# A new hand-written order for the 1648 operations of an attention and gated feed-forward kernel

## The chip, the core and the metric

The kernel runs on one core of a Trainium2 chip. The core has five engines that each work through a queue of their own, in order: TensorE (PE, matrix products; PEld is its loading of weights), VectorE (DVE), ScalarE (ACT), GpSimd (POOL) and SyncE (SP, which here only issues transfers). They wait for one another through semaphores. The metric is the device time of one execution in microseconds. The kernel before takes 346.71 us (median of 3 runs, 345.82 to 346.75).

## The reference

```
for c in range(nc):                                   # 24 chunks of 32 queries
    q_c = q[:, :, c_start:c_end]
    k_full = concat([mem_k, k[:, :, l_start:r_end]])  # 8 memory keys, 16 left, 32 own, 8 right
    scores = scale * matmul(q_c, k_full.T)
    a = exp(scores - max);  a = a / (sum(a) + 1e-9)
    out[:, :, c_start:c_end] = matmul(a, v_full)
x = out, heads joined                                 # (4, 768, 512)
h = maximum(x @ w_in, 0)                              # (4, 768, 1024)
conv = sum over k of conv_w[k] * h shifted by k - 1   # three taps along the sequence
y = (h * sigmoid(conv)) @ w_out                       # (4, 768, 512)
```

Four batches of 768 positions, 8 heads of 64. The weights arrive as 64-bit floats; every product of the feed-forward part is made of three products of a high and a low part, so that it has nearly the precision of fp32.

## The kernel before, in words

The work is cut into 1648 operations. Function `op` of class `Plan` records each with what it reads and writes; the functions below it (`from_f64`, `attention`, `ffn_in`, `gated`, `sums`, `weight_sums`, `seven`, `ffn_out`) only make operations. At the end `run` goes through the list `ORDER` and issues them in exactly that order. Each engine gets its operations in the order in which the list names them, so the one list sets all five queues, and it also decides which buffer a tile gets: a tile takes the first free slot of its pool at its first use, and gives it back after its last.

- `from_f64` (L296 to L364) turns one block of 64-bit weights into a high and a low fp32 part, on ACT, DVE and partly POOL. It has run 17 times when all weights are there.
- `attention` runs 32 times (4 batches, 2 halves of the sequence, 4 pairs of heads). PE makes the scores (L397, tile `s`), DVE takes their maximum (L406, tile `top`). Then either DVE subtracts it (L411) and ACT takes the exponential (L417), or ACT scales the maximum (L428) and takes six exponentials with it as a bias (L432). DVE sums (L444) and inverts (L446), DVE or POOL multiplies (L449). The result is turned, either by PE (L461) or by DVE and a trip through DRAM (L479, tile `t_dram`); ACT copies it (L468), PE multiplies it with v (L508, tile `ta`), and ACT and DVE split that into high and low parts (L511, L514).
- `ffn_in` is 64 times four groups of three PE products (L530, tile `f`), with a copy by ACT (L540) that applies the maximum with zero.
- `gated` is 32 times the three taps (ACT L551 or DVE L555, then DVE L560 twice), a tanh on ACT (L564), the product with h (DVE L569, or ACT L573 and POOL L574), and the split of the result (ACT L586, then DVE or POOL L589).
- `ffn_out` makes 18 of the 24 output tiles: 24 PE products each (L727), a copy by ACT (L738) and a store. The last batch goes another way: `sums` and `weight_sums` prepare sums of its operands and of the output weights (L596, L644), and `seven` makes seven block products in place of eight (L680, L698).

`weight_sums` is ten operations on POOL at L596, numbers 1298 to 1307 in the list, each over 128x1024 elements. They can run as soon as all of w_out is converted, and they are needed only by the last batch.

Of the kernel before, what the change touches and what calls it, by code (L numbers as in the profile page):

```python
# [46 lines left out]
    581, 582, 570, 571, 12, 587, 588, 583, 584, 11, 14, 28, 572, 573, 29, 585, 576, 592, 574, 45, 46, 589, 575, 15,  # L47
    16, 586, 17, 31, 63, 62, 13, 48, 79, 598, 32, 30, 80, 577, 33, 18, 19, 34, 20, 21, 22, 47, 602, 64, 35, 578,
    579, 36, 65, 593, 96, 590, 49, 23, 37, 50, 38, 97, 580, 24, 39, 51, 594, 595, 52, 53, 54, 40, 131, 25, 41, 66,
    67, 596, 82, 599, 591, 42, 26, 68, 69, 600, 27, 130, 597, 43, 601, 70, 756, 71, 612, 44, 739, 603, 114, 83, 55,  # L50
    773, 56, 58, 113, 740, 622, 57, 72, 73, 147, 165, 604, 605, 606, 607, 84, 608, 75, 74, 774, 757, 85, 81, 76,
    59, 609, 86, 60, 87, 99, 148, 88, 77, 610, 133, 61, 758, 775, 98, 100, 613, 101, 741, 134, 78, 166, 135, 89,
    90, 618, 619, 611, 791, 792, 92, 643, 91, 102, 632, 136, 793, 794, 742, 795, 116, 115, 614, 615, 759, 103, 616,
    617, 620, 104, 621, 743, 0, 776, 105, 106, 132, 808, 809, 810, 811, 623, 628, 117, 118, 119, 624, 120, 107,
    108, 150, 629, 625, 200, 626, 630, 137, 151, 93, 631, 812, 199, 138, 649, 139, 627, 140, 218, 168, 109, 110,
    94, 358, 111, 95, 287, 760, 121, 826, 122, 112, 169, 827, 828, 829, 141, 778, 183, 123, 633, 124, 143, 777,
    634, 635, 125, 126, 170, 638, 813, 182, 814, 796, 797, 830, 127, 1, 636, 2, 637, 152, 142, 144, 217, 393, 202,
    153, 639, 154, 640, 641, 128, 129, 145, 146, 642, 203, 744, 171, 745, 235, 644, 645, 3, 4, 779, 780, 149, 5,
    650, 6, 7, 204, 155, 8, 9, 646, 205, 647, 172, 206, 815, 816, 156, 781, 782, 798, 173, 817, 207, 648, 799, 800,
    157, 208, 158, 10, 209, 159, 201, 185, 186, 651, 652, 220, 236, 187, 818, 801, 210, 211, 783, 746, 221, 831,  # L60
    832, 833, 174, 222, 802, 803, 161, 761, 762, 763, 819, 784, 820, 188, 189, 804, 160, 764, 747, 748, 749, 765,
    175, 252, 805, 167, 176, 253, 834, 867, 868, 664, 238, 835, 836, 162, 849, 862, 184, 239, 288, 844, 845, 163,
    377, 766, 178, 837, 863, 213, 846, 847, 767, 190, 191, 864, 865, 177, 848, 179, 750, 192, 212, 240, 255, 290,
    322, 271, 665, 821, 850, 851, 869, 675, 430, 241, 242, 768, 180, 769, 852, 270, 243, 870, 340, 342, 164, 949,
    256, 853, 244, 181, 866, 223, 871, 193, 195, 666, 950, 272, 751, 219, 838, 257, 670, 305, 785, 671, 224, 289,
    194, 1002, 1003, 324, 214, 752, 258, 196, 822, 215, 273, 259, 341, 245, 216, 197, 854, 872, 985, 986, 198, 225,
    274, 880, 881, 786, 839, 246, 951, 676, 823, 952, 953, 323, 260, 667, 1004, 226, 882, 306, 681, 227, 228, 229,
    840, 275, 883, 673, 884, 1005, 682, 375, 987, 897, 988, 668, 677, 678, 679, 248, 261, 291, 989, 262, 292, 293,
    263, 237, 931, 898, 932, 230, 684, 294, 295, 264, 855, 276, 277, 278, 231, 254, 899, 841, 900, 933, 296, 787,
    279, 280, 1006, 247, 934, 343, 325, 376, 753, 683, 326, 249, 360, 232, 250, 344, 914, 327, 233, 915, 265, 916,  # L70
    251, 685, 901, 359, 234, 281, 770, 328, 885, 886, 935, 266, 919, 283, 856, 345, 329, 412, 330, 672, 771, 331,
    917, 297, 298, 308, 346, 857, 282, 267, 674, 653, 361, 858, 268, 284, 309, 299, 918, 332, 285, 333, 334, 824,
    362, 363, 990, 991, 269, 286, 481, 347, 348, 394, 669, 954, 955, 411, 654, 364, 788, 301, 956, 957, 992, 349,
    920, 300, 887, 655, 888, 889, 890, 310, 311, 873, 921, 659, 336, 993, 350, 902, 903, 904, 656, 905, 906, 335,
    351, 302, 657, 907, 660, 874, 661, 658, 958, 891, 892, 396, 378, 697, 337, 922, 908, 303, 698, 967, 968, 662,
    994, 875, 972, 973, 859, 410, 969, 365, 312, 366, 970, 974, 975, 663, 313, 314, 338, 893, 352, 315, 703, 1007,
    339, 316, 704, 699, 1008, 1009, 772, 429, 971, 894, 976, 923, 463, 307, 936, 318, 317, 379, 380, 937, 397, 398,
    381, 382, 959, 354, 876, 353, 938, 428, 383, 413, 355, 399, 384, 385, 386, 400, 1010, 304, 939, 940, 395, 414,
    415, 1011, 1124, 401, 356, 941, 1020, 416, 464, 367, 368, 319, 357, 466, 320, 700, 701, 431, 321, 686, 692,
    1089, 680, 960, 687, 1021, 693, 369, 705, 371, 402, 706, 924, 1022, 1141, 387, 370, 445, 482, 1090, 702, 1091,  # L80
    909, 961, 389, 719, 432, 1023, 433, 417, 688, 1092, 1093, 388, 1125, 1126, 1024, 842, 1127, 1055, 1056, 535,
    1057, 1012, 962, 390, 418, 419, 446, 448, 720, 942, 420, 910, 943, 372, 1013, 1058, 1037, 421, 1128, 963, 877,
    391, 449, 422, 860, 1059, 1072, 1038, 403, 392, 404, 1073, 450, 406, 721, 722, 373, 944, 964, 945, 725, 925,
    1039, 1040, 806, 405, 374, 708, 499, 1106, 1107, 946, 1108, 1109, 1074, 423, 695, 1014, 689, 789, 790, 690,
    1075, 1015, 434, 467, 694, 1142, 1143, 1144, 407, 1076, 424, 425, 408, 1016, 484, 1145, 707, 1041, 426, 1129,
    1130, 427, 409, 1111, 995, 807, 1060, 1061, 451, 911, 825, 1017, 723, 691, 843, 1062, 1063, 696, 1112, 1064,
    996, 452, 1110, 724, 453, 1113, 1131, 1132, 1133, 1025, 1114, 926, 1115, 468, 754, 729, 1094, 1095, 755, 1096,
    1097, 454, 1026, 455, 435, 436, 714, 1027, 1028, 1077, 1368, 1029, 735, 927, 726, 1098, 928, 437, 727, 1078,
    485, 456, 457, 1079, 1146, 977, 978, 730, 1030, 486, 438, 709, 710, 517, 736, 1042, 487, 1043, 1044, 731, 732,
    1045, 711, 1080, 895, 712, 439, 1046, 728, 878, 518, 1147, 440, 713, 733, 1148, 1369, 1370, 1149, 1388, 737,  # L90
    738, 1371, 488, 861, 447, 997, 1081, 1378, 1389, 458, 516, 459, 469, 470, 471, 441, 734, 1116, 472, 1379, 1380,
    1381, 1382, 979, 498, 1150, 715, 717, 519, 520, 716, 718, 1298, 460, 442, 483, 501, 1390, 1391, 521, 522, 523,
    524, 525, 1392, 1383, 1384, 1358, 1359, 1117, 465, 998, 879, 929, 1099, 999, 473, 1118, 502, 503, 474, 461,
    475, 476, 1372, 462, 1385, 553, 526, 1373, 1299, 1300, 1386, 489, 527, 1360, 1361, 1362, 1363, 1364, 504, 505,
    1365, 506, 1100, 1031, 1366, 490, 1032, 1374, 1398, 1348, 1349, 534, 980, 477, 981, 1399, 1400, 443, 491, 1401,
    1402, 1350, 1375, 1151, 1403, 1101, 552, 444, 1387, 1152, 1065, 492, 1367, 1376, 493, 1351, 965, 528, 555, 478,
    494, 495, 529, 537, 530, 1153, 1176, 507, 508, 1033, 1066, 1352, 1404, 1405, 1353, 1354, 1082, 966, 1377, 479,
    947, 1102, 1177, 509, 538, 539, 1406, 1407, 496, 540, 541, 480, 1281, 1178, 556, 948, 1119, 497, 896, 912,
    1355, 557, 1083, 1084, 510, 512, 982, 1356, 983, 984, 1393, 1394, 1134, 913, 1047, 1048, 558, 559, 1135, 1228,
    1179, 1229, 1230, 1282, 1283, 542, 543, 536, 1103, 511, 1180, 560, 1159, 1160, 1395, 1161, 1120, 1121, 1231,  # L100
    1000, 1284, 1085, 1162, 1163, 1086, 500, 561, 562, 513, 1285, 1232, 531, 1396, 1397, 544, 1246, 1247, 563, 930,
    564, 1248, 1438, 1193, 514, 1357, 1210, 545, 546, 1049, 1211, 1249, 515, 1212, 1439, 1440, 1154, 1050, 1441,
    1442, 1194, 1443, 1051, 565, 1155, 1067, 1250, 1018, 566, 1195, 1001, 532, 1052, 1196, 1264, 1265, 1266, 1267,
    1197, 548, 554, 1444, 1418, 533, 1268, 1136, 1156, 1301, 1419, 1420, 1137, 567, 547, 549, 1304, 550, 1019,
    1445, 1138, 551, 568, 569, 1198, 1421, 1068, 1213, 1199, 1446, 1251, 1200, 1201, 1214, 1447, 1202, 1215, 1216,
# [759 lines left out]
```

## Time and profile before

| | |
|---|---|
| median of 3 runs | 346.71 us |
| the profiled execution | 346.62 us, its span 344.8 us |
| mean granted clock of TensorE | 0.995 |
| PE busy | 328.1 us, 95% of the span |
| DVE busy | 279.3 us, 81% |
| ACT busy | 209.7 us, 61% |
| POOL busy | 117.4 us, 34% |

PE has work in nearly all of the span. A matrix product is counted busy from its start to its end, and products overlap, so PE's busy time says less than the distance from one start to the next. Where a row ends in square brackets, they hold the idle time of the engine just before the instruction and what ended it. The durations of DVE and POOL hold the time in which an instruction had begun and stood still.

### The profile page before, as it was taken

To read this page: it belongs to the slowest core of one execution; us is meant where nothing else is said; L and a number is where in the kernel's file an instruction comes from. 1 tells how busy PE (TensorE), PEld (TensorE's weight loads), DVE (VectorE), ACT (ScalarE), POOL (GpSimd) and SP (SyncE) were. 2 spreads that over 40 slices of the span, in tenths; PEclk is the share of its full clock that TensorE was granted. 3 is DMA by queue.
4 is the path that set the end of the run, shared out by engine and by line. 5 is a ranking of instruction groups with operands and counts; after the bars stand their busy time and mean duration, and the time that the engine had idled before them with its cause. 6 is when DMAs were issued, how large, how long until landed. Compare 5 with 4: busy or idle time off the path is not lost.

```text
span 344.8 us, 7675 instructions
## 1 busy us (share of the span) xinstructions
PE 328.1 (95%) x3039; PEld 298.5 (87%) x3039; DVE 279.3 (81%) x452; ACT 209.7 (61%) x438; POOL 117.4 (34%) x95
## 2 busy tenths in 40 slices
PE   0789999999999999999998999999999999999996
PEld 0679999999999999999885799989998888889995
DVE  4999979989988999799889997973769848798432
ACT  4587778878879688968734377543238781545000
POOL 2524221133361422521093324299600694000100
PEclk9999999999999999999999899999999999999999
DMA  7999955999785971502620733320000010012022
GB/s 270 402 398 400 374 233 183 318 389 338 236 280 175 292 218 55 144 33 60 201 93 24 228 108 116 127 72 30 3 30 0 33 61 30 32 61 91 32 77 77
DMA packets 27107, 54.52 MB, mean 158 GB/s; under 512 B 3136, under 2 KB 14528, under 8 KB 27072
## 3 DMA queue, kind: packets, MB, share of 16 engines
q1 hardware_dynamic: 27072, 54.04, 45.1%
q8 instruction: 24, 0.39, 0.4%
q14 instruction: 11, 0.09, 0.1%
HBM read 44.79 MB, written 9.24 MB: 157 GB/s over the span
## 4 chain that ended last, share of the span: by engine, by line
PE 88%; DVE 4%; ACT 3%; DMA 2%; issue 1%; SPq 1%; POOL 0%; ACTq 0%
PE f L530 40%; PE f L727 26%; PE ta L508 6%; PE s L397 6%; PE f L680 4%; PE s L680 2%; PE ta L680 2%; DMA w<-in_w_in_dram 2%; PE ta L461 2%; DVE u L569 1%; ACT a_d L468 1%; ACT e L432 1%; SPq L277 1%; DVE top L406 1%; DVE u L560 1%
## 5 line engine op out<-in xcount | busy, mean ns | idle before, releaser
L530 PE MATMUL f<-u,w_in_hi 128*128 128x384 f32 x512 | 141.5, 344 | 0.5 <-DVE u L514 0.5
L727 PE MATMUL f<-w_out_hi,u 128*128 128x512 f32 x288 | 95.8, 401 | 1.6 <-ACT w_top L738 1.6
L530 PEld LDWEIGHTS f<-u,w_in_hi 128*128 128x128 f32 x512 | 93.2, 188 | 3.0 <-DVE u L514 1.2
L530 PE MATMUL f<-u,w_in_lo 128*128 128x384 f32 x256 | 86.3, 337 | 0.0
L560 DVE SCALAR_TENSOR_TENSOR u<-u,cw,u 128x767 f32<-128x767 f32 x64 | 70.8, 1125 | 0.4
L727 PEld LDWEIGHTS f<-w_out_hi,u 128*128 128x128 f32 x288 | 55.0, 191 | 14.8 <-ACT w_top L738 2.5
L727 PE MATMUL f<-w_out_lo,u 128*128 128x512 f32 x144 | 57.6, 400 | 0.0
L530 PEld LDWEIGHTS f<-u,w_in_lo 128*128 128x128 f32 x256 | 48.1, 188 | 0.6
L540 ACT ACTIVATE u<-f 128x384 f32<-128x384 f32 x64 | 30.5, 491 | 29.7 <-PE f L530 28.7
L589 DVE TENSOR_TENSOR u<-u,u 128x768 fp32r<-128x768 f32 (+1 forms) x32 | 35.3, 1116 | 13.9 <-ACT u L586 11.6
L449 POOL TENSOR_TENSOR e<-e,z 128x384 f32<-128x384 f32 x21 | 21.7, 1034 | 61.5 <-DVE z L446 39.5
L574 POOL TENSOR_TENSOR u<-u,u 128x768 f32<-128x768 f32 x15 | 30.7, 2058 | 24.7 <-ACT u L573 24.7
L589 POOL TENSOR_TENSOR u<-u,u 128x768 fp32r<-128x768 f32 (+1 forms) x8 | 17.2, 2165 | 61.6 <-ACT u L586 38.1
L564 ACT ACTIVATE u<-u 128x768 f32<-128x768 f32 x32 | 27.0, 848 | 12.2 <-DVE u L560 12.2
L586 ACT CAST u<-u 128x768 fp32r<-128x768 f32 (+1 forms) x40 | 31.4, 803 | 2.3 <-DVE u L596 2.2
L727 PEld LDWEIGHTS f<-w_out_lo,u 128*128 128x128 f32 x144 | 27.4, 190 | 5.7
L569 DVE SCALAR_TENSOR_TENSOR u<-u,u 128x768 f32<-128x768 f32 x17 | 25.3, 1488 | 0.0
L397 PE MATMUL s<-k,u 128*64 128x64 f32 x672 | 23.8, 223 | 0.7 <-DMA k<-in_k_dram 0.7
L397 PEld LDWEIGHTS s<-k,u 128*64 128x64 f32 x672 | 21.5, 138 | 3.2 <-issue 2.4
L738 ACT COPY w_top<-f 128x512 f32<-128x512 f32 x18 | 10.6, 588 | 21.9 <-PE f L727 15.2
L551 ACT ACTIVATE u<-u,cw 128x768 f32<-128x768 f32 x23 | 21.1, 936 | 2.6 <-PE f L727 2.5
L514 DVE TENSOR_TENSOR u<-ta,u 128x384 fp32r<-128x384 f32 x32 | 17.0, 546 | 6.2 <-ACT u L511 6.2
(94 smaller groups left out, 496.3 us busy)
## 6 DMA issues: line engine op xcount, KB each, us to landing
u<-in_q_dram SPq DMA_DIRECT2D x32, 384.0 KB, 6.3
u<-in_v_dram SPq DMA_DIRECT2D x25, 384.0 KB, 6.7
k<-in_k_dram SPq DMA_DIRECT2D x28, 252.0 KB, 5.5
out_dram<-w_top SPq DMA_DIRECT2D x18, 256.0 KB, 2.0
w<-in_w_in_dram SPq DMA_DIRECT2D x8, 512.0 KB, 7.4
w<-in_w_out_dram SPq DMA_DIRECT2D x8, 512.0 KB, 5.3
t_dram<-w SPq DMA_DIRECT2D x15, 192.0 KB, 1.9
a_d<-t_dram SPq DMA_DIRECT2D x30, 96.0 KB, 3.8
```

Source lines behind the costliest of these rows:

```text
L397: nc.tensor.matmul(s.t[j * D : (j + 1) * D, o : o + KW], lhsT=q_[:, c], rhs=k_t.t[:, c * STEP : c * STEP + KW], start=True, stop=True,)
L449: lambda: (V if norm == "V" else G).tensor_tensor(out=keys(e), in0=keys(e), in1=pairs(z.t).unsqueeze(3).broadcast_to([P, NG, 2, KW]), op=A ...
L530: nc.tensor.matmul(f.t[:, :TW], lhsT=w_in_p[c][:, fc, cc], rhs=x.t[:, a * TW : (a + 1) * TW], start=(cc == 0 and i == 0), stop=(cc == NCC ...
L540: "A", act(TW, True), lambda: A.activation(h.t[:, hf * TW : (hf + 1) * TW], f.t[:, :TW], AF.Relu, scale=0.5), (f,), ((h, hf),)
L560: lambda j=j, to=to, at=at: V.scalar_tensor_tensor(out=c.t[:, to], in0=h.t[:, at], scalar=w[j], in1=c.t[:, to], op0=ALU.mult, op1=ALU.add) ...
L564: plan.op("A", act(S), lambda: A.activation(c.t, c.t, AF.Tanh), (c,), (c,), table="exp")
L569: lambda: V.scalar_tensor_tensor(out=y.t, in0=c.t, scalar=1.0, in1=h.t, op0=ALU.add, op1=ALU.mult),
L574: plan.op("G", 2.42 * S, lambda: G.tensor_tensor(out=y.t, in0=c.t, in1=h.t, op=ALU.mult), (c, h), (y,), shared=True)
L586: plan.op("A", act(n), lambda: A.copy(out=hi(), in_=src()), (y,), (k_hi,))
L589: lambda: (V if eng == "V" else G).tensor_tensor(out=low(), in0=src(), in1=hi().bitcast(F32), op=ALU.subtract),
L680: nc.tensor.matmul(ps.t[:, :n], lhsT=l[a](), rhs=w[c], start=(j == 0 and m == 0), stop=(j == hf - 1 and m == 2))
L727: nc.tensor.matmul(ps.t[:, :n], lhsT=gs[b, fc][a].t[:, tt * P : (tt + 1) * P], rhs=w_out_p[c][:, fc, o : o + n], start=(fc == 0 and i == 0 ...
```

## The change

Only the list `ORDER` is replaced: the same 1648 numbers in another order. No operation, tile, engine or size changes. Two lines of each list, where they name the first operations of `weight_sums`:

```diff
 ORDER = [
...
-    524, 525, 1392, 1383, 1384, 1358, 1359, 1117, 465, 998, 879, 929, 1099, 999, 473, 1118, 502, 503, 474, 461,
-    475, 476, 1372, 462, 1385, 553, 526, 1373, 1299, 1300, 1386, 489, 527, 1360, 1361, 1362, 1363, 1364, 504, 505,
...
+    1382, 1402, 486, 1364, 1365, 1366, 1367, 462, 928, 1403, 1390, 1404, 1405, 1383, 1384, 1406, 1298, 1407, 554,
...
+    1372, 1049, 1373, 1102, 556, 511, 496, 542, 543, 1154, 480, 530, 512, 1050, 529, 1299, 1247, 544, 513, 497,
...
 ]
```

What it does to the queues is shown at three places.

POOL, where the weight sums (L596) begin. `w` are buffers for weights, `e` the exponentials of the attention, `u` tiles of the feed-forward part. Before:

```order
L449 TENSOR_TENSOR e_76<-e_76,z_99 128x3x128
L439 MEMSET e_74 64x16
L359 TENSOR_TENSOR w_out_lo<-w_92 128x512
L596 TENSOR_TENSOR w_90<-w_out_hi 128x1024
L449 TENSOR_TENSOR e_74<-e_74,z_102 128x3x128
L596 TENSOR_TENSOR w_90<-w_90,w_out_lo 128x1024 x2
L449 TENSOR_TENSOR e_75<-e_75,z_101 128x3x128
```

and now:

```order
L359 TENSOR_TENSOR w_out_lo<-w_92 128x512
L449 TENSOR_TENSOR e_76<-e_76,z_102 128x3x128
L596 TENSOR_TENSOR w_89<-w_out_hi 128x1024
L449 TENSOR_TENSOR e_76<-e_76,z_101 128x3x128
L574 TENSOR_TENSOR u_1566<-u_1829,u_1566 128x768
L596 TENSOR_TENSOR w_89<-w_89,w_out_lo 128x1024
L449 TENSOR_TENSOR e_74<-e_74,z_99 128x3x128
L439 MEMSET e_75 64x8
L574 TENSOR_TENSOR u_2135<-u_2135,u_1401 128x768
L596 TENSOR_TENSOR w_89<-w_89,w_out_lo 128x1024
L596 TENSOR_TENSOR w_91<-w_out_hi,w_89 128x1024
```

The first three L596 stood within four instructions; now other work stands between the first, the second and the third, and the fourth follows the third directly. In the list, operation 1298 (the first L596) has gone from place 1003 to place 1049, 1300 (the third) from 1042 to 1185, and 1307 (the last) from 1346 to 1278.

ACT, where the copies of finished output tiles (L738) stand behind a scaled maximum (L428). Before:

```order
L564 ACTIVATE u_2098<-u_2098 128x768
L586 CAST u_2420<-u_1462 128x768
L428 ACTIVATE top_95<-top_95 128x6
L511 CAST u_2430<-ta_105 128x384
L738 COPY w_top_93<-f_107 128x512
L432 ACTIVATE e_74<-s_104,top_95 128x64 x6
L738 COPY w_top_94<-f_110 128x512
```

and now:

```order
L511 CAST u_2414<-ta_106 128x384
L428 ACTIVATE top_98<-top_98 128x6
L738 COPY w_top_93<-f_108 128x512
L738 COPY w_top_94<-f_110 128x512
L551 ACTIVATE u_2476<-u_1987,cw 128x768
L432 ACTIVATE e_76<-s_103,top_98 128x64 x6
L551 ACTIVATE u_2493<-u_1923,cw 128x768
L586 CAST u_2506<-u_1366 128x768
L738 COPY w_top_93<-f_107 128x512
L428 ACTIVATE top_95<-top_95 128x6
```

A scaled maximum still stands ahead of the first copies, but another one. The maximum that it waits for, DVE's L406, was operation 502 at place 1029 of the list, behind the first L596; now it is operation 485 at place 1017, ahead of the first L596 at 1049, and so is the next one (538, place 1003).

DVE at the start of the program, its instructions 16 to 24 before:

```order
L444 TENSOR_REDUCE z_99<-e_74 128x6
L446 RECIPROCAL z_99<-z_99 128x6
L449 TENSOR_TENSOR e_74<-e_74,z_99 128x3x128
L444 TENSOR_REDUCE z_100<-e_75 128x6
L406 TENSOR_REDUCE top_97<-s_103 128x6
L446 RECIPROCAL z_100<-z_100 128x6
L411 TENSOR_TENSOR e_76<-s_103,top_97 128x3x128
L449 TENSOR_TENSOR e_75<-e_75,z_100 128x3x128
L296 TENSOR_SCALAR w_top_93<-w_top_93 128x512
```

and its instructions 16 to 24 now:

```order
L444 TENSOR_REDUCE z_99<-e_74 128x6
L296 TENSOR_SCALAR w_top_93<-w_top_93 128x512
L302 TENSOR_SCALAR w_top_93<-w_top_93 128x512
L406 TENSOR_REDUCE top_97<-s_103 128x6
L446 RECIPROCAL z_99<-z_99 128x6
L411 TENSOR_TENSOR e_76<-s_103,top_97 128x3x128
L449 TENSOR_TENSOR e_74<-e_74,z_99 128x3x128
L444 TENSOR_REDUCE z_100<-e_75 128x6
L406 TENSOR_REDUCE top_98<-s_104 128x6
```

Four instructions (L296, L302, L406, L411) have moved ahead of the first L449, whose result PE turns first. Further up, the ten instructions that DVE runs on the first weights are the same ten, but L317 and L322, which need only the load, stood first, and now L296 does, which needs ACT's L292. On PE, one more set of scores (L397) stands ahead of the first L530: six, where it was five.

## Rows read from the trace of the kernel before

**Rows 1.** The page's first part: busy us, share, instructions.

```profile
PE 328.1 (95%) x3039; PEld 298.5 (87%) x3039; DVE 279.3 (81%) x452; ACT 209.7 (61%) x438; POOL 117.4 (34%) x95
```

**Rows 2.** Stretches: length, busy us of PE, PEld, DVE, ACT, POOL, clock, DMA share, GB/s.

```profile
0.00:20.00 20.00, 8.71 (x176) 7.58 (x176) 14.44 (x31) 11.10 (x25) 7.93 (x22) 1.00 0.90 346
...
176.00:193.00 17.00, 15.38 (x59) 11.70 (x58) 16.31 (x18) 5.50 (x14) 8.77 (x5) 0.90 0.22 70
...
220.00:260.00 40.00, 40.00 (x246) 36.84 (x246) 26.94 (x25) 14.75 (x27) 22.77 (x9) 1.00 0.15 50
```

**Rows 3.** The same view, a shorter stretch.

```profile
189.00:192.40 3.40, 3.40 (x9) 2.62 (x8) 3.36 (x6) 1.75 (x4) 0.64 (x1) 0.50 0.72 216
```

**Rows 4.** PE by time, 185 to 193 us: start, us, instruction, idle before.

```profile
185.70 0.40 PE L727 MATMUL f<-w_out_hi,u 128*128 128x512 f32 x1
186.97 0.50 PE L727 MATMUL f<-w_out_hi,u 128*128 128x512 f32 x1 [0.87 <-ACT w_top L738]
...
187.53 0.39 PE L727 MATMUL f<-w_out_hi,u 128*128 128x512 f32 x1
188.68 0.53 PE L727 MATMUL f<-w_out_hi,u 128*128 128x512 f32 x1 [0.76 <-ACT w_top L738]
...
192.67 0.39 PE L727 MATMUL f<-w_out_lo,u 128*128 128x512 f32 x1
```

**Rows 5.** The chain that ended last: start, us, what.

```profile
256.95 48.29 PE f L727 x207
```

**Rows 6.** ACT by time, at the same place.

```profile
185.85 0.21 ACT L428 ACTIVATE top<-top 128x6 f32<-128x6 f32 x1 [9.86 <-DVE top L406]
...
186.33 0.59 ACT L738 COPY w_top<-f 128x512 f32<-128x512 f32 x1
```

**Rows 7.** DVE by time, 174 to 186 us.

```profile
175.13 2.06 DVE L560 SCALAR_TENSOR_TENSOR u<-u,cw,u 128x767 f32<-128x767 f32 x1
177.11 1.58 DVE L589 TENSOR_TENSOR u<-u,u 128x768 fp32r<-128x768 f32 x1
178.73 2.63 DVE L555 TENSOR_SCALAR u<-u,cw 128x768 f32<-128x768 f32 x1
181.28 3.14 DVE L569 SCALAR_TENSOR_TENSOR u<-u,u 128x768 f32<-128x768 f32 x1
...
185.28 0.55 DVE L406 TENSOR_REDUCE top<-s 128x6 f32<-128x384 f32 x1
```

**Rows 8.** POOL by time, 170 to 184 us.

```profile
173.97 2.40 POOL L596 TENSOR_TENSOR w<-w_out_hi 128x1024 f32<-128x1024 f32 x1
...
177.84 5.77 POOL L596 TENSOR_TENSOR w<-w,w_out_lo 128x1024 f32<-128x1024 f32 x2
```

**Rows 9.** All instructions of a line: shortest, median, longest ns, first and last start.

```profile
L560 DVE SCALAR_TENSOR_TENSOR u<-u,cw,u x64: 973/1012/2603, 57.1 to 295.2; 128x767 f32<-128x767 f32 x64
L589 DVE TENSOR_TENSOR u<-u,u x32: 551/951/3166, 142.7 to 321.7; 128x768 fp32r<-128x768 f32 x30, 128x384 fp32r<-128x384 f32 x2
L555 DVE TENSOR_SCALAR u<-u,cw x9: 609/621/2633, 178.7 to 260.1; 128x768 f32<-128x768 f32 x9
L569 DVE SCALAR_TENSOR_TENSOR u<-u,u x17: 918/952/3160, 62.2 to 309.8; 128x768 f32<-128x768 f32 x17
L596 POOL TENSOR_TENSOR w<-w,w_out_lo x6: 2409/2596/3101, 177.8 to 244.2; 128x1024 f32<-128x1024 f32 x6
```

**Rows 10.** DVE by time, 4 to 15 us.

```profile
4.55 0.43 DVE L317 TENSOR_SCALAR w<-w 128x512 uint32<-128x512 uint32 x1 [4.55 <-DMA w<-in_w_in_dram]
...
9.77 0.56 DVE L406 TENSOR_REDUCE top<-s 128x6 f32<-128x384 f32 x1 [0.51 <-PE s L397]
...
13.27 0.56 DVE L449 TENSOR_TENSOR e<-e,z 128x384 f32<-128x384 f32 x1
```

**Rows 11.** ACT by time, its first instruction on data.

```profile
4.55 0.69 ACT L292 ACTIVATE w_top<-w 128x512 f32<-128x512 f32 x1 [2.54 <-DMA w<-in_w_in_dram]
```

**Rows 12.** PE by time, its first L530.

```profile
19.59 0.44 PE L530 MATMUL f<-u,w_in_hi 128*128 128x384 f32 x1
```

158 rows, old and new, of the table ORDER are left out of this document.

## The prediction

> **What bounds the kernel now.** I read the page's first part, then the windows, then PE's timeline where a window shows it short of work, then what released PE there, engine by engine.
>
> The first part names PE: 328.1 us busy, where DVE has 279.3 and ACT 209.7 [rows 1]. Against the span of 344.8 us that leaves PE 16.7 us idle. The windows show where: 20.00 − 8.71 = 11.29 us lie in the first 20, in which DVE is busy 14.44 us, that is 14.44 of the 15.45 that are left to it once its first data are there at 4.55; and 17.00 − 15.38 = 1.62 us lie between 176 and 193 [rows 2, 10]. All the rest of the span, its tail included, holds 16.7 − 11.29 − 1.62 = 3.8 us. So an order that keeps the products as they are can win in two places: at the start, which DVE bounds, and in one stretch in the middle.
>
> In the middle the loss is larger than the idle time. Undisturbed, the products follow each other at 48.29 / 207 = 0.233 us [rows 5]. Here one start lies 186.97 − 185.70 = 1.27 us behind the last, another 188.68 − 187.53 = 1.15 us; both times PE waits (0.87 and 0.76 us) for a copy of a finished tile, L738, that empties the bank it wants to write [rows 4]. Right after that the granted clock is 0.50 over 3.40 us, the lower level, 1.2 GHz [rows 3]: PE had been idle twice within 2 us before it fell. The ten steps from 188.68 to 192.67 take 3.99 us where ten at 0.233 take 2.33 [rows 4, 5]. The excess is 1.27 − 0.23 = 1.04, 1.15 − 0.23 = 0.92, and 3.99 − 2.33 = 1.66, together 3.62 us.
>
> Followed back: the copies stand in ACT's queue behind L428, which had waited 9.86 us for DVE's L406 and ran at 185.85; the first copy follows at 186.33 [rows 6]. L406 itself ran at 185.28, because DVE was late [rows 7]. DVE was late because four instructions ahead of it took far longer than their line takes: L560 2.06 against a median of 1.01 us, L589 1.58 against 0.95, L555 2.63 against 0.62, L569 3.14 against 0.95 [rows 7, 9]. The excesses are 1.05 + 0.63 + 2.01 + 2.19 = 5.88 us. Each of the four lies beside an L596 on POOL: one from 173.97 for 2.40 us, two from 177.84 for 5.77 [rows 8]. L555 shows how: begun at 178.73, inside the first of that pair, which by half of 5.77 ends at 180.73, it ends at 181.36, its own 0.62 us after that. It stood still while GpSimd worked.
>
> **The change, part by part.** No instruction is added or taken away; durations come from the profiled execution (346.62 us, of which 1.82 lie around the span), 0.09 below the median of 346.71.
>
> (a) The middle. The maximum that L428 and the copies behind it wait for now stands ahead of the first L596 in the list, the next one too, and L449 and L574 stand between the first three L596. Take away the 5.88 us and DVE, busy 16.31 of 17.00 us [rows 2], has 0.69 + 5.88 = 6.57 us of slack in that stretch; the maximum would come by about 185.28 − 5.88 = 179.4. PE's first idle moment was at 186.10 (185.70 + 0.40) [rows 4], so L428, L738 and PE would be in time by more than 5 us. The two waits go, and the stretch at half clock that followed them: −3.62 us. What is late next: the copies have DVE's other maxima ahead of them still, and the later L596 fall beside L555 and L569 elsewhere. That costs PE nothing as long as PE has other work, and it had some here: L428 began to wait at 185.85 − 9.86 = 175.99 [rows 6], PE ran dry 10.1 us later. If this cover is gone the price is again 1 us a wait and 1.66 for the clock. Bounds of this part: −3.62, and 0 if the same wait comes back elsewhere.
>
> By the Trainium skill, SBUF — State Buffer, section "Who interferes with whom", the pair of ports that VectorE and GpSimd share is a lock: whoever issues first has it for the whole of its instruction, and the other stands still. The trace agrees, with 2.63 us for an L555 of 0.62. The rule speaks against this change as much as for it: ten L596 hold the lock as long in any order, and spreading them only changes who stands behind them; by it DVE would win nothing in sum, and the time would hang on which DVE result PE wants next.
>
> (b) The seven later L596. Before, they too cost DVE time: L589 and L569 reach 3.17 and 3.16 us [rows 9]. Yet from 220 to 260, where POOL is busy 22.77 us and L596 runs until after 244.2, PE is busy 40.00 of 40.00 [rows 2, 9]. Nothing is to be gained there: 0. What it may cost where they stand now is the third rival.
>
> (c) The start. DVE's first instruction was L317, at 4.55, on data alone [rows 10]. Now it is L296, which needs ACT's L292, from 4.55 to 5.24 [rows 11]: 0.69 us later. DVE's wait of 0.51 us ahead of its L406 at 9.77 [rows 10] then vanishes, which leaves +0.18. Further, four instructions go ahead of the first L449 (13.27), whose result PE turns first. At the longest of these durations, 0.56 us [rows 10], they put it back by at most 2.24 us, and the first L530 (19.59) [rows 12] with it, if nothing else were to do. But they are work that has to be done in any case for the weights and the scores that come next, and PE has one more set of scores to do in between. Bounds: −0.51 (the wait goes and the 0.69 hides) to 0.18 + 2.24 = +2.42. I take +0.18, since DVE bounds this stretch (14.44 of 15.45 us) and does the same work in it in either order.
>
> Sum: 346.62 − 3.62 + 0.18 = 343.18, and 0.09 more on the median: **343.3 us**. With the bounds of (c) and up to 0.9 us of (a) given back it lies between 342.5 and 344.9; a quarter of the 3.8 us that PE idles elsewhere, if the new order saves that too, makes the lower end 341.5.
>
> **The rivals.** *First: the start costs its bound.* The four moved instructions count in full: 346.71 − 3.62 + 2.42 = 345.5 us. For it speaks that PE is idle 11.29 of the first 20 us and hangs on DVE there; against it, that the same DVE instructions are paid back a little later. It is still faster, barely.
>
> *Second: no change.* The wait moves instead of going: ACT takes its queue in order, some L428 still stands ahead of copies, and one late maximum stops PE twice, with the half clock behind it. Then −3.62 becomes 0 and the time is 346.71 + 0.18 = 346.9 us; with the start hidden, 346.7. For it speaks that DVE's sum of work and of stalls is as large; against it, that both first maxima now stand ahead of every L596.
>
> *Third: slower.* Of the ten L596 only the third and fourth are now neighbours among the first four, and L574 and L449 bring POOL's queue to them while DVE still owes PE the last sets of the attention. If six of them stop a DVE instruction that PE's path needs, at 2.01 to 2.19 us each (L555, L569) [rows 7, 9], DVE loses 6 × 2.1 = 12.6 us there. Before, 5.88 us lost by DVE became 3.62 on PE, 0.62 each: 12.6 × 0.62 = 7.8 us, and 346.71 + 0.18 − 3.62 + 7.8 = 351.1. It decides from the point where PE's waits and the clock behind them come to 3.62 − 0.18 + 1.04 = 4.5 us, that is three waits of 1 us and one stretch at half clock. For it: DVE is nearly full in such a stretch (16.31 of 17.00). Against it: PE had 10 us of other work here, and lost nothing to the later L596 [rows 2].
>
> **How the numbers follow.** A measurement of this kernel tells about 0.3% (1.04 us) from no change: faster is below 345.67, slower above 347.75. Forecast 0.60, first rival 0.13, second 0.13, third 0.14. The forecast and most of the first rival are faster, 0.72; the second and what is left of the first are the same, 0.14; slower is 0.14. The range of 8 in 10 goes from 341.5, the low end of the forecast, over the first rival to the second: 346.9.
>
> **What would show it.** (a) is right if the profile after has no PE wait of 0.7 us or more on an L738 with a following stretch at clock 0.50 in the middle, and PE's starts there lie 0.233 us apart; it is wrong if such a stretch stands anywhere between 150 and 260. (b) is right if PE is busy all of the windows that hold the later L596, though DVE's L555, L560, L569 and L589 still show 2 to 3 us there. (c) shows at DVE's first instruction, about 5.3, and the first L530: by 20.5 the small price holds, at 22 the first rival. The whole is wrong if PE gains in the middle and loses as much between 24 and 150, where I expect no change.

## The result, and the profile after

The new order takes 343.31 us (median of 5 runs, 342.45 to 344.27), the old one 346.71; the ratio is 0.9907, 95% interval 0.9883 to 0.9932. The forecast was 343.3. The profiled span fell from 344.8 to 341.0 us. The first part of the page, against [rows 1]:

```profile
PE 327.5 (96%) x3039; PEld 298.7 (88%) x3039; DVE 285.5 (84%) x452; ACT 210.7 (62%) x438; POOL 112.9 (33%) x95
```

DVE is busy 6.2 us longer than before with the same instructions, and the kernel is 3.4 us shorter: DVE stands still longer beside GpSimd (below: it loses time to the port that the two share), but elsewhere. The same three windows as in [rows 2]:

```profile
0.00:20.00 20.00, 10.20 (x176) 8.81 (x178) 13.86 (x31) 10.35 (x24) 8.21 (x22) 1.00 0.93 346
176.00:193.00 17.00, 17.00 (x74) 13.67 (x73) 15.31 (x23) 9.24 (x25) 3.10 (x2) 1.00 0.43 141
220.00:260.00 40.00, 40.00 (x241) 35.94 (x240) 37.88 (x30) 16.17 (x26) 23.13 (x9) 1.00 0.04 14
```

Between 176 and 193 PE is now busy throughout, at full clock: the 1.62 us of idle time and the stretch at 0.50 [rows 2, 3] are gone. From 220 to 260 DVE is busy 37.88 us where it was 26.94, with GpSimd's sums beside it, and PE still has work in all 40. The chain of waits after, in order of time (start, us, what), against [rows 5], has PE at its products without a break over the time of the old stall:

```profile
168.03 25.19 PE f L727 x108
193.55 2.81 PE f L727 x12
```

25.19 / 108 = 0.233 us, the undisturbed step. On DVE (start, us, instruction, idle before; against [rows 7]) one instruction, L302, stood still beside an L596 in this stretch, and the awaited maximum, L406, came at 181.51:

```profile
175.17 0.55 DVE L406 TENSOR_REDUCE top<-s 128x6 f32<-128x384 f32 x1
175.63 2.29 DVE L302 TENSOR_SCALAR w_top<-w_top 128x512 uint32<-128x512 uint32 x1
...
181.51 0.55 DVE L406 TENSOR_REDUCE top<-s 128x6 f32<-128x384 f32 x1
```

L302 takes 0.43 us at the program's start and 2.29 here, beside the one L596 on POOL (against [rows 8], where three stood within 10 us):

```profile
175.23 2.40 POOL L596 TENSOR_TENSOR w<-w_out_hi 128x1024 f32<-128x1024 f32 x1 [2.70 <-DMA t_dram<-w]
189.58 1.47 POOL L449 TENSOR_TENSOR e<-e,z 128x384 f32<-128x384 f32 x1 [11.94 <-DVE z L446]
196.24 2.02 POOL L574 TENSOR_TENSOR u<-u,u 128x768 f32<-128x768 f32 x1 [5.19 <-ACT u L573]
198.23 2.39 POOL L596 TENSOR_TENSOR w<-w,w_out_lo 128x1024 f32<-128x1024 f32 x1
```

The second L596 now starts 23 us after the first. On ACT, against [rows 6], L428 waited 2.41 us for L406, not 9.86, and the copy behind it ran at 182.21, not 186.33:

```profile
182.09 0.21 ACT L428 ACTIVATE top<-top 128x6 f32<-128x6 f32 x1 [2.41 <-DVE top L406]
182.21 0.57 ACT L738 COPY w_top<-f 128x512 f32<-128x512 f32 x1
```

The start, against [rows 10 to 12], first on DVE, then on PE:

```profile
5.06 0.43 DVE L296 TENSOR_SCALAR w_top<-w_top 128x512 f32<-128x512 f32 x1 [5.06 <-ACT w_top L292]
...
15.01 0.55 DVE L449 TENSOR_TENSOR e<-e,z 128x384 f32<-128x384 f32 x1
```

```profile
20.76 0.45 PE L530 MATMUL f<-u,w_in_hi 128*128 128x384 f32 x1
```

L449 comes 1.74 us later and the first L530 1.17 us later, but PE is busy 10.20 us of the first 20, where it was 8.71.

Where the gain lies can be estimated from the two traces. Each product of PE is given the usual distance from one start to the next of its kind (0.233 us for L727, 0.174 for L530, about 0.026 for L397 and L508), and the work that both orders have done by the same moment is compared. By this estimate the new order is 0.3 us ahead at 24 us, 0.6 ahead at 150 and 0.1 behind at 184; at 204 it is 3.2 us ahead, and at the end 3.8. Nearly all of the gain is made between 184 and 204 us, and what PE was busier at the start is not kept.

### The profile page after: what moved, and what is told of

Its sections match the earlier page's. It is cut to its first block, busy times and chain, and to the rows that moved or that the text cites. A ratio compares the mean times of both kernels' runs of the same rounds, so it can differ in the third digit from the quotient of the medians.

```text
span 341.0 us, 7681 instructions
## 1 busy us (share of the span) xinstructions
PE 327.5 (96%) x3039; PEld 298.7 (88%) x3039; DVE 285.5 (84%) x452; ACT 210.7 (62%) x438; POOL 112.9 (33%) x95
## 4 chain that ended last, share of the span: by engine, by line
PE 87%; DVE 4%; DMA 4%; ACT 3%; issue 1%; SPq 0%; DVEq 0%
PE f L530 35%; PE f L727 30%; PE ta L508 6%; PE s L397 6%; PE f L680 4%; DMA u<-in_k_dram 4%; PE ta L680 3%; PE s L680 2%; PE ta L461 2%; DVE u L560 1%; ACT e L432 1%; DVE top L406 1%; ACT u L540 1%; ACT u L564 0%; DVE u L514 0%
## 5 line engine op out<-in xcount | busy, mean ns | idle before, releaser
L530 PE MATMUL f<-u,w_in_hi 128*128 128x384 f32 x512 | 140.1, 343 | 0.4 <-ACT u L540 0.3
L530 PEld LDWEIGHTS f<-u,w_in_hi 128*128 128x128 f32 x512 | 93.2, 188 | 2.8 <-ACT u L540 1.1
L727 PE MATMUL f<-w_out_hi,u 128*128 128x512 f32 x288 | 92.6, 396 | 0.0
L530 PE MATMUL f<-u,w_in_lo 128*128 128x384 f32 x256 | 86.1, 336 | 0.0
L560 DVE SCALAR_TENSOR_TENSOR u<-u,cw,u 128x767 f32<-128x767 f32 x64 | 72.4, 1143 | 0.3
L727 PEld LDWEIGHTS f<-w_out_hi,u 128*128 128x128 f32 x288 | 54.1, 188 | 12.5
L727 PE MATMUL f<-w_out_lo,u 128*128 128x512 f32 x144 | 56.9, 395 | 0.0
L589 DVE TENSOR_TENSOR u<-u,u 128x768 fp32r<-128x768 f32 (+1 forms) x32 | 42.7, 1353 | 10.4 <-ACT u L586 4.4
L530 PEld LDWEIGHTS f<-u,w_in_lo 128*128 128x128 f32 x256 | 48.1, 188 | 0.3
L449 POOL TENSOR_TENSOR e<-e,z 128x384 f32<-128x384 f32 x21 | 19.4, 926 | 54.1 <-DVE z L446 47.5
L727 PEld LDWEIGHTS f<-w_out_lo,u 128*128 128x128 f32 x144 | 27.1, 188 | 6.0
L589 POOL TENSOR_TENSOR u<-u,u 128x768 fp32r<-128x768 f32 (+1 forms) x8 | 14.7, 1848 | 41.2 <-ACT u L586 32.1
L397 PEld LDWEIGHTS s<-k,u 128*64 128x64 f32 x672 | 21.5, 138 | 2.9 <-issue 2.2
L397 PE MATMUL s<-k,u 128*64 128x64 f32 x672 | 24.0, 224 | 0.1
L569 DVE SCALAR_TENSOR_TENSOR u<-u,u 128x768 f32<-128x768 f32 x17 | 21.0, 1234 | 1.7 <-ACT u L564 1.7
L738 ACT COPY w_top<-f 128x512 f32<-128x512 f32 x18 | 10.4, 585 | 18.0 <-PE f L727 15.2
```

What stands on the lines that cost most here:

```text
L397: nc.tensor.matmul(s.t[j * D : (j + 1) * D, o : o + KW], lhsT=q_[:, c], rhs=k_t.t[:, c * STEP : c * STEP + KW], start=True, stop=True,)
L530: nc.tensor.matmul(f.t[:, :TW], lhsT=w_in_p[c][:, fc, cc], rhs=x.t[:, a * TW : (a + 1) * TW], start=(cc == 0 and i == 0), stop=(cc == NCC ...
L560: lambda j=j, to=to, at=at: V.scalar_tensor_tensor(out=c.t[:, to], in0=h.t[:, at], scalar=w[j], in1=c.t[:, to], op0=ALU.mult, op1=ALU.add) ...
L569: lambda: V.scalar_tensor_tensor(out=y.t, in0=c.t, scalar=1.0, in1=h.t, op0=ALU.add, op1=ALU.mult),
L589: lambda: (V if eng == "V" else G).tensor_tensor(out=low(), in0=src(), in1=hi().bitcast(F32), op=ALU.subtract),
L727: nc.tensor.matmul(ps.t[:, :n], lhsT=gs[b, fc][a].t[:, tt * P : (tt + 1) * P], rhs=w_out_p[c][:, fc, o : o + n], start=(fc == 0 and i == 0 ...
```

## The experiments

Eleven kernels, each timed in five rounds beside the old order on the same chip. The old order's own median was 345.87 to 346.47 us there, so kernels are compared by their ratios to it. All but one change only the list; where the list became one line shorter, line numbers are one less, so that L405, L427, L448, L559, L568 and L737 there are L406, L428, L449, L560, L569 and L738 above.

**The third sum alone moved.**

```diff
-    ..., 1373, 1299, 1300, 1386, 489, ...
+    ..., 1373, 1299, 1386, 489, ...
...
-    ..., 1136, 1156, 1301, 1419, ...
+    ..., 1136, 1156, 1300, 1301, 1419, ...
```

> The order of before, with the third L596 alone (operation 1300) moved behind the stretch, directly ahead of operation 1301. Theory A (one late maximum: PE loses nothing until its cover is used up, then all of it): the L569 at 181.28 keeps its 0.95 us, the awaited L406 runs near 183.1 in place of 185.28, ACT's first copy near 184, before PE needs it at 186.1; the whole 3.6 us go, 343.1 us, though two L596 still stop DVE there. Rival B (in proportion: 0.62 us of PE for each us that DVE loses there): only 2.19 x 0.62 = 1.4 us go, 345.3. Rival C (the gain came from the new order as a whole, and the L596 beside it are incidental): 346.7.

Measured 343.55 us, ratio 0.9924 (0.9908 to 0.994). DVE then PE:

```profile
178.39 2.64 DVE L554 TENSOR_SCALAR u<-u,cw 128x768 f32<-128x768 f32 x1
180.95 0.95 DVE L568 SCALAR_TENSOR_TENSOR u<-u,u 128x768 f32<-128x768 f32 x1
181.82 1.01 DVE L559 SCALAR_TENSOR_TENSOR u<-u,cw,u 128x767 f32<-128x767 f32 x1
182.75 0.55 DVE L405 TENSOR_REDUCE top<-s 128x6 f32<-128x384 f32 x1
```

```profile
196.15 0.92 PE L507 MATMUL ta<-a_d,u 128*64 128x64 f32 x24 [0.83 <-ACT a_d L467]
```

One L596 fewer in the stretch gives back 2.6 us of the 3.6. C falls, and so does B with its price of 0.62. A had the place right, but not the rest: a wait of 0.83 us stands at 196, which no theory had and which the trace of the old order does not show.

**All three moved.**

```diff
-    ..., 716, 718, 1298, 460, ...
+    ..., 716, 718, 460, ...
...
-    ..., 1136, 1156, 1301, 1419, ...
+    ..., 1136, 1156, 1298, 1299, 1300, 1301, 1419, ...
```

> The order of before, with the first three L596 (1298 to 1300) moved directly ahead of 1301, so that all ten come late. Theory A: 343.1 us, no PE wait between 176 and 193, and no loss at the ten later ones. Rival B: DVE loses as much at ten later ones as it did at three and seven, PE loses in proportion there, 345 to 347. Rival C: 346.7.

Measured 347.0 us, ratio 1.0021 (1.0004 to 1.0037). The two waits near 187 went, 0.76 us at 196.8 came, and ten L596 between 225 and 253 made another. ACT and PE:

```profile
254.02 0.84 ACT L585 CAST u<-u 128x768 fp32r<-128x768 f32 x1 [5.91 <-DVE u L568]
...
259.22 0.84 ACT L563 ACTIVATE u<-u 128x768 f32<-128x768 f32 x1 [3.60 <-DVE u L559]
...
260.69 0.48 ACT L539 ACTIVATE u<-f 128x384 f32<-128x384 f32 x1
```

```profile
196.81 0.92 PE L507 MATMUL ta<-a_d,u 128*64 128x64 f32 x24 [0.76 <-ACT a_d L467]
...
261.23 0.49 PE L726 MATMUL f<-w_out_hi,u 128*128 128x512 f32 x1 [2.16 <-ACT u L539]
```

DVE, which lost the port to them (an L568 of 3.15 us at 250.84), kept ACT waiting 5.91 and 3.60 us, and the L539 behind, which empties a bank of `f`, came too late for PE. That is the mechanism of the third rival, at a place where the old order had not paid. The time would fit rival B, but PE did not pay in proportion: by their durations DVE's instructions lost some 14 us to the ten L596, and PE fell back by 2.7 us there (the same estimate as above, from 240 to 280 us).

**The awaited maximum alone moved.**

```diff
-    ..., 1359, 1117, 465, ..., 473, 1118, 502, 503, ...
+    ..., 1359, 502, 1117, 465, ..., 473, 1118, 503, ...
```

> The order of before, all L596 left where they are, with the one awaited L406 (operation 502) moved ahead of the L560 that runs at 175.13. Its scores were there at 174.0. Theory A: DVE still loses 5 to 6 us to the three L596, with L555 and L569 of 2 to 3 us, but L406 runs near 175.1, ACT's L428 and L738 come in time, and the 3.6 us go: 343.1. Rival B (DVE's lost time itself is what PE pays for): 346.7. Rival C: 346.7.

Measured 345.69 us, ratio 0.999 (0.9977 to 1.0002). ACT:

```profile
176.37 0.20 ACT L427 ACTIVATE top<-top 128x6 f32<-128x6 f32 x1
184.93 0.48 ACT L510 CAST u<-ta 128x384 fp32r<-128x384 f32 x1 [8.35 <-DVE u L568]
185.31 0.59 ACT L737 COPY w_top<-f 128x512 f32<-128x512 f32 x1
```

L427 ran 9.5 us earlier, and nothing clear of the noise was won: the L510 behind it waits for DVE's late L568 (181.75 to 184.89), so the first copy came only 1 us earlier, and PE still waited 1.01 us for a copy and 1.19 us for L467 at 198.7. Theory A in the form "one late maximum" falls.

**The copies ahead of both waits.**

```diff
-    ..., 502, 503, 474, 461, 475, 476, 1372, 462, ..., 1300, 1386, ..., 504, 505, ..., 506, ..., 1366, 490, ...
+    ..., 502, 474, 475, 476, 1372, ..., 1300, 1386, ..., 1366, 503, 461, 462, 504, 505, 506, 490, ...
```

> The order of before, every L596 and every DVE instruction up to the awaited L406 left where it is. On ACT the two copies L738 (operations 1386 and 1366) now stand ahead of L428 and of the L511 behind it, where they stood behind both; what hangs on these two (the exponentials, two instructions of DVE behind L406, the split of L514) follows them. Theory A, mended after the run in which the maximum alone was moved (ACT then waited at L511, so 0.5 us at most were won): PE pays for ACT's place in line and not for what DVE loses; L560, L589, L555 and L569 still take 5.9 us more than their lines do, ACT copies near 180.6 and 185.5, PE waits for no L738, and 2.6 us (if PE then waits 1.0 us near 196, as with the third sum moved) to 3.6 us go: 0.990 to 0.9925 of before. Rival B (what DVE loses is what PE pays): 1.000.

Measured 346.0 us, ratio 0.9993 (0.9977 to 1.0009). PE waited for no copy, but it waited three times later on, 2.81 us in all:

```profile
193.05 0.55 PE L460 MATMUL ta<-ident,e 128*128 128x128 f32 x3 [0.58 <-POOL e L448]
195.31 0.92 PE L396 MATMUL s<-k,u 128*64 128x64 f32 x24 [1.02 <-DMA u<-in_q_dram]
...
198.15 0.92 PE L507 MATMUL ta<-a_d,u 128*64 128x64 f32 x24 [1.21 <-ACT a_d L467]
```

SyncE's queue and ACT show why (SPq is SyncE's sequencer):

```profile
185.71 0.33 SPq L485 DMA_DIRECT2D t_dram<-w  x1
...
188.98 0.43 SPq L276 DMA_DIRECT2D u<-in_q_dram  x1
...
190.76 0.85 SPq L741 DMA_DIRECT2D out_dram<-w_top  x2
```

```profile
195.91 0.59 ACT L737 COPY w_top<-f 128x512 f32<-128x512 f32 x1 [5.98 <-DMA out_dram<-w_top]
196.39 0.47 ACT L467 COPY a_d<-ta 64x384 f32<-64x384 f32 x1
```

The store L485 needs DVE's turning L478, which DVE reached at 185.11. SyncE issues in order, so behind it stood the loads of q and the stores of finished tiles, copied at 180 and 185 but issued at 190.76. The next copy found no free tile until 195.91, and L467, which PE wanted, stood behind that. A falls in its mended form too, and the ratio is the one that B had. But not all of this delay is DVE's: with all three sums moved L485 had left at 180.85, and the two stores still left only at 189.74, behind loads of q that waited for PE.

**What is wanted first, and the elementwise work after.**

```diff
-    ..., 929, 1099, 999, 473, 1118, 502, 503, 474, 461, 475, ..., 462, ..., 527, 1360, ...
+    ..., 929, 473, 502, 503, 474, 475, ..., 527, 1099, 999, 1118, 461, 462, 1360, ...
```

> The order of before with every L596 left where it is. On DVE the three elementwise instructions L555, L569 and L560 (operations 1099, 999, 1118) go behind the awaited L406, both L479 (474, 527), whose stores hold up SyncE's queue, and an L449; the split L511 and L514 (461, 462) follows them. Theory D (formed after two runs in which the waits on L738 went and others came 5 to 12 us later: what DVE owes is wanted by several queues, SyncE's through L479 among them, and PE pays when its nearest creditor is late): DVE still loses 4 to 6 us to the three L596, but what is wanted comes by 182 in place of 185 to 188; the out stores leave 3 to 4 us earlier; PE loses under 1.5 us between 180 and 200 in place of 3.8: 0.9925 to 0.995 of before. Rival B (what DVE loses there PE pays, in any order): 0.998 to 1.001.

Measured 344.56 us, ratio 0.9952 (0.9937 to 0.9968), every L596 where it was. DVE and SyncE:

```profile
178.51 0.55 DVE L405 TENSOR_REDUCE top<-s 128x6 f32<-128x384 f32 x1
178.98 0.56 DVE L478 STREAM_TRANSPOSE w<-e 128x384 f32<-128x384 f32 x1
179.47 1.79 DVE L448 TENSOR_TENSOR e<-e,z 128x384 f32<-128x384 f32 x1
```

```profile
179.57 0.33 SPq L485 DMA_DIRECT2D t_dram<-w  x1
...
189.90 0.85 SPq L741 DMA_DIRECT2D out_dram<-w_top  x2
```

L485 left 6.8 us and the out stores 3.2 us earlier than in the old order (186.33 and 193.06 there). PE's waits fell to 0.38 and 0.80 us. The ratio is at the edge of D's range (0.9925 to 0.995). But DVE also lost less here, since L405 and L478 ran beside the sums at their own length: 4.07 us against 5.88. So D is supported in its result, but not separated from B. With 1300 moved as well:

> The same, with the third L596 (1300) moved behind the stretch as well. If both remedies add up, PE loses under 0.5 us between 180 and 200: 0.989 to 0.991 of before, as the new order. If what is left is the store of a finished tile that ACT's next copy waits for (PE waited 1.0 us near 196 with the third sum moved), 0.992 as there.

Measured 344.04 us, ratio 0.9937 (0.9917 to 0.9956): the remedies do not add up, and a wait near 196 stays (0.47 us), as the second case of the expectation had it.

**The sums put together again in the new order.**

```diff
-    ..., 1384, 1406, 1298, 1407, ..., 529, 1299, 1247, ..., 548, 1300, 565, ...
+    ..., 1384, 1406, 1298, 1299, 1300, 1407, ..., 529, 1247, ..., 548, 565, ...
```

> The new order, with the second and third L596 (1299, 1300) moved directly behind the first (1298). POOL then runs them from about 175 to 183, as before, and the awaited L406 that ran at 181.51 stands behind the DVE instructions that they stop. Theory A (threshold): L309 and one or two more lose some 2 us each, L406 comes about 4.3 us late, near 186; the bank that the first L738 empties had 3.3 us to spare (ready at 182.8, wanted at 186.1), so PE waits about 1 us on L738 and the clock may fall behind it: 343.3 + 1.0 to + 2.7, that is 344.3 to 346. Rival B (in proportion, 0.62 for each us lost by DVE): 4.3 x 0.62 = 2.7, 346.0, with no one place where PE waits. Rival C (the new order as a whole has the gain): 343.3.

Measured 348.02 us, ratio 1.0069 (1.0051 to 1.0087), slower than the old order. DVE and PE:

```profile
175.84 2.30 DVE L301 TENSOR_SCALAR w_top<-w_top 128x512 uint32<-128x512 uint32 x1
178.17 2.76 DVE L308 SCALAR_TENSOR_TENSOR w_top<-w,w_top 128x512 uint32<-128x512 uint32 x1
180.97 2.46 DVE L327 TENSOR_SCALAR w<-w_top 128x512 uint32<-128x512 uint32 x1
183.46 0.69 DVE L363 SCALAR_TENSOR_TENSOR w_out_lo<-w 128x512 fp32r<-128x512 uint32 x1
```

```profile
181.64 0.50 PE L726 MATMUL f<-w_out_hi,u 128*128 128x512 f32 x1 [0.76 <-ACT w_out_hi L313]
...
184.21 0.50 PE L726 MATMUL f<-w_out_lo,u 128*128 128x512 f32 x1 [2.06 <-DVE w_out_lo L363]
```

All three theories missed size and place: the stopped instructions here (2.30, 2.76 and 2.46 us, where the same lines usually take 0.43, 0.69 and 0.42) convert the last block of w_out, which PE multiplies by next. The clock was 0.57 from 185 to 189. This one edit takes away the whole gain and more.

**The new order without the sums' work.**

```diff
-            add(next(e), hf * n, lambda: t(k), raw[k], a, b, r, op)
+            if raw[k] in r:
+                add(next(e), 16, lambda: t(k)[:, :, :16], raw[k], lambda: a()[:, :, :16], lambda: b()[:, :, :16], r, op)
+            else:
+                plan.op(next(e), 400, lambda: G.memset(t(k), 1.0), r, (raw[k],))
```

> The new order without the work of the ten L596: four of them only fill their tile with ones, six work on 16 of 256 columns of each block, so the last batch's output is not the reference's. It asks what the L596 still cost the new order. Theory A: DVE's instructions beside them fall back to 0.6 to 1.0 us, DVE busy falls by about 20 us, and the time stays within 0.3 us of 343.3, since PE never waited. Rival B (PE pays for lost DVE time in proportion): 20 x 0.62 = 12 us less, or at least a clear gain of over 1 us.

Measured 342.39 us, ratio 0.9912 (0.9889 to 0.9936), as the new order with its sums. DVE busy fell to 268.0 us, by 17.5. B falls. Where the sums now stand they cost nothing that can be measured (the interval is 0.8 us to either side).

**The two starts.** The first 150 operations of one order, then the rest in the sequence of the other.

> The first 150 operations of the new order, then the other operations in the order of before: the new start alone (up to some 25 us), with the stall in the middle as before. The small price of the start: 346.71 + 0.18 = 346.9 us. The four moved instructions counted in full (first rival): 349.1. What the profile after suggests, where PE is 0.35 us ahead at 40 us: 346.4. In each of them PE waits twice on L738 near 187 and the clock falls there; if the start alone took that stall away, the reason for the middle would be wrong.

Measured 348.36 us, ratio 1.0055 (1.0037 to 1.0074). By its size this is near the first rival (349.1 / 346.71 = 1.0069). But PE lost it behind the seam and not at the start: by the estimate above it is level with the old order at 30 us and 1.0 us behind at 40, with a wait for a block of w_in in between:

```profile
31.99 0.44 PE L529 MATMUL f<-u,w_in_lo 128*128 128x384 f32 x1 [0.68 <-POOL w_in_lo L351]
```

The middle showed two waits on L737 again, 1.6 us in sum. The mirror decides whether the new start is a price in the order that it was made for.

> The mirror of the run with the new start: the first 150 operations in the old order, then the others in the new one. If the start weighs nothing (what the windows of both profiles show up to 40 us), 0.990 to 0.992 of before; if the seam between the two orders costs as it did there (1.4 us near 32 us), 0.994 to 0.996; if the new start was itself a price that the new order pays, under 0.990.

Measured 343.13 us, ratio 0.9909 (0.9879 to 0.9939): with the old start the new order is as fast, to about 1 us.

**Two copies earlier in the new order.**

```diff
-    ..., 962, 963, 964, 1150, ..., 439, 980, ..., 806, 1043, 1029, ...
+    ..., 962, 1150, 963, 964, ..., 439, 1029, 980, ..., 806, 1043, ...
```

> The new order with two of ACT's L540 moved ahead: operation 1150 ahead of the L573 at 153.27, 1029 ahead of the L564 at 154.39; their products had been finished 2.5 and 4.6 us before ACT copied them. In the profile after, PE's starts lose 0.28 and 0.42 us there. If PE pays only where a bank is late, 343.3 - 0.7 = 342.6; if the copies put ahead make the tanh or the split behind them late for something else, no change or slower.

Measured 342.78 us, ratio 0.9911 (0.9893 to 0.9928). PE is busy 20.00 of 20 us from 140 to 160, where it had 19.62 in the new order, but 18.97 from 80 to 100, where it had 20.00 and the list is the same. Not to be told from the new order; no kernel here is clearly faster than that.

## Why the prediction was right, and where it was not

The total and its sign were right. That 343.3 was met so closely is luck: five runs lie between 342.45 and 344.27, the old order's median was 345.87 to 346.47 us in the later sessions where it had been 346.71, and two errors in term (a), on the clock and on the waits, partly cancel. The terms:

(a) 3.62 us for the middle. The size held: PE has no wait there and no half clock, and it gains 3.3 us between 184 and 204. The reason was half right. The step that failed is "the maximum that L428 and the copies behind it wait for now stands ahead of the first L596": that alone is worth nothing that can be measured (0.999), nor are copies freed from their waits (0.9993). The other half of the sentence, other work between the L596, carries the gain: one L596 moved away gives 0.9924, and together again they undo it (1.0069). What the prediction missed stands under "what is late next": behind the maximum, DVE also owed L511's tile, the turning L479 that SyncE's store waits for, and with it a part of what stands behind in SyncE's queue. These runs set what DVE lost to the port between 174 and 184 (its longer durations less the usual ones) beside PE's waits of over 0.3 us from 176 to 200:

| order | DVE lost, us | PE waits, us | ratio |
|---|---|---|---|
| before | 5.88 | 1.63, then half clock | 1 |
| copies ahead | 5.86 | 2.81 | 0.9993 |
| maximum ahead | 5.44 | 2.20 | 0.999 |
| wanted first | 4.07 | 1.18 | 0.9952 |
| third sum later | 3.71 | 0.83 | 0.9924 |
| wanted first, third sum later | 2.91 | 0.5 | 0.9937 |
| all three sums later | 0 | 0.76 | 1.0021, with 2.16 us lost at 261 |
| new order | 1.86 | 0 | 0.9907 |
| new order, sums together | 5.98 | 2.82, then half clock | 1.0069 |

PE's waits fall with DVE's backlog, whichever instruction is moved, but not to nothing. With all three sums moved DVE lost nothing here, PE gained 2.5 us between 184 and 204 where the new order gains 3.3, and a wait of 0.76 us was left. This rest is not DVE's. ACT's next copy of a finished tile begins at 194.57, when the store of an older tile has landed (194.50); that store stands in SyncE's queue behind loads that wait for PE; and L467, which PE wants, stands behind the copy on ACT. In the new order the two stores leave at 184.03, where the old order with all three sums moved has them at 189.74, and both L468 stand ahead of the copy; SyncE, then ACT:

```profile
184.03 1.13 SPq L742 DMA_DIRECT2D out_dram<-w_top  x2
```

```profile
193.58 0.47 ACT L468 COPY a_d<-ta 64x384 f32<-64x384 f32 x1 [0.61 <-PE ta L461]
...
196.19 0.58 ACT L738 COPY w_top<-f 128x512 f32<-128x512 f32 x1
```

So about 2.5 us of the gain hang on the sums, and about 0.8 us on places in ACT's and SyncE's queues that the prediction does not name. That these places are the reason for the 0.8 is read from the traces; no run moved them alone.

The clock term of 1.66 was too large. With the copies ahead the clock never fell, and PE waited 2.81 us instead, later. In 45 of the 64 timed executions of the old order beside these kernels the mean granted clock was 0.998 or more, where one stretch of 3.40 us at half clock makes 0.995; they took 346.06 us in the mean, the 19 others 346.61. The run with the new start and the old rest had the two waits at full clock, and between 184 and 204 it lost only 0.7 us less than the trace of the old order, for there PE waited another 0.65 us on L467 at 199.88. The clock was worth some 0.6 us, and the wait on L467 stood behind it. The 3.62 was right as the whole of what PE lost in the traced execution, not as three separate prices.

(b) Nothing for the seven later L596: right for both orders, though PE's cover there has an end: ten in a row ended in a wait of 2.16 us.

(c) +0.18 for the start. Measured, nothing that stands out of 1 us of noise: old start and new rest give 0.9909, and PE is level with the old order at 184 us. Between 24 and 150, where no change was expected, PE is busy 125.93 of 126 us, as before (125.92). The first L530 came at 20.76, between the two marks set for it; that mark was poor, since PE did other work before it.

Of the rivals, the first (start at its bound) and the second (the wait moves) did not happen, but the second is what every repair of one wait alone ran into. The third did not happen in this order, and did in two of the experiments.

## What to carry to other kernels

When an engine that others wait for falls behind, take away what holds it up; freeing the one result that shows as the wait only brings the next creditor forward, often through a queue that was not looked at (here SyncE's). List everything that the late engine owes before pricing a repair, and look for what stands behind each wait: a wait that goes, or a clock that does not fall, may only uncover the next one. A long GpSimd instruction may cost DVE time without costing the kernel, if several do not stand together ahead of something PE wants soon.

## What the runs showed of the hardware

The half clock did not follow each pair of short waits. Before, waits of 0.87 and 0.76 us within 2 us were followed by 3.40 us at 0.50 [rows 3, 4]; in the run with the new start and the old rest two such waits (0.87 and 0.75 us) were followed by full clock (columns as in [rows 2]):

```profile
188.00:190.00 2.00, 0.96 (x3) 0.49 (x3) 1.58 (x4) 2.00 (x9) 0.00 (x0) 1.00 0.28 102
190.00:192.00 2.00, 1.90 (x8) 1.59 (x9) 1.90 (x5) 1.97 (x4) 0.00 (x0) 1.00 0.40 68
192.00:194.00 2.00, 2.00 (x10) 1.59 (x10) 2.00 (x5) 0.98 (x2) 0.81 (x1) 1.00 0.97 346
```

The old order itself mostly ran without such a stretch: 45 of its 64 timed executions had a mean granted clock of 0.998 or more, the others 0.990 to 0.995.

DVE's L406 and L479 kept their usual 0.55 and 0.56 us beside an L596 (in the run with what is wanted first, at 178.51 and 178.98, where a pair of L596 began at 177.73 and took 5.78 us), while L302, L309, L328, L449, L555, L560, L569 and L589 stood still in one run or another.

That spreading the sums saves DVE nothing was said ahead, from the Trainium skill (SBUF — State Buffer, "Who interferes with whom"): whichever of the two engines issues first holds the shared port for its whole instruction, in any order of the list. The trace agrees: DVE's busy time did not fall, it rose from 279.3 to 285.5 us.
